# Moving the edge rows of a causal convolution from TensorE to Pool, with a rearranged start

## The chip, the cores and the metric

One core of a Trainium2 chip. The metric is the device time of one execution in microseconds (us), as the median over several runs. A program that is alone on its core has no second core to compare with, so the granted TensorE clock that each run reports is kept beside its time. A run more than 1.5% above the fastest of its kernel would count as slow and be left out. Profiles are single executions.

## The reference, cut to what matters

A lightweight causal convolution of seven taps (softmax-normalised weights, one set for each of 8 heads) is followed by a two-layer block with a cosine gate.

```python
# x (8, 4096, 192), weight (8, 7), w_in (192, 2048), w_out (2048, 192)
w = softmax(weight)                       # cut: max, exp, sum + 1e-9
x_unf = zero_padded(x)[:, idx, :]         # the row itself and the six before it
conv  = einsum('hk,bskhg->bshg', w, x_unf)    # 24 channels a head
h     = conv.reshape(32768, 192) @ w_in
out   = (h * cos(h)) @ w_out
```

## The kernel before

Tokens are taken in 64 tiles of 512; two tiles make a unit of 1024, 32 units in all. Within a tile TensorE computes eight pairs of hidden blocks (`h0` to `h7`, 6 matmuls of 512 columns each), ACT takes the cosine (`s0` to `s7`, a sine with a shifted phase), DVE multiplies, and 64 output steps (`m`, pairs of 192-column matmuls) of an earlier tile are threaded between. The convolution of a later unit (`c`, `d`) is done by TensorE with a banded matrix, in blocks of 128 tokens. The first six tokens of a block need rows of the block before it. A unit therefore has a ninth block, `UB`, into which the 16 rows around each block boundary are loaded, convolved along with the others, and copied over the wrong columns afterwards:

```python
def conv_mm(u, c, ps, i, rows, n0, n1, prev=0, **flags):        # cut
    rhs = bf[u][rows, n0:n1, h * G : (h + 1) * G]     # n1 = UB + 1: 9 blocks x 24 = 216 columns

def double_unit(u, n0=0, n1=UB + 1):                  # Pool
    nc.gpsimd.tensor_copy(out=ct[:, n0:n1, :, 1, :], in_=ct[:, n0:n1, :, 0, :])

def turn_unit(u, ...):                                # SyncE issues DMA transposes ct -> cT
def mend_edges(u):                                    # Pool, once the transposes have landed
    nc.gpsimd.tensor_copy(out=cT[u][:, 0:UB, :, 0 : K - 1],
                          in_=cT[u][:, UB]....[:, :, :, 8 : 8 + K - 1])
```

Once a unit, Pool does: mend unit u+1, cast unit u+3, double unit u+2, in this order. The first four tiles have orders of their own; this is tile 1 (`p` and `q` are the points where output banks change, and after `q` a matmul waits for a marker that SyncE passes on in its own queue):

```python
PE_ORDER  = "h0 m1 c1 m6 c2 m4 h1 m10 h2 p h3 m10 h4 m9 h5 m9 h6 m4 q h7 m11"
PE_FIRST[1] = "p m4 h0 m1 h1 m5 h2 m6 h3 m12 h4 m2 h5 m2 q m1 d1 d2 m4 h6 m6 c1 c2 m3 h7 m3"
```

## Time and profile before

| quantity | value |
|---|---|
| time | 715.81 us median of 3 runs (715.52 to 716.16) |
| TensorE busy | 704.0 of 714.0 us |
| DVE, ACT, Pool busy | 91%, 84%, 21% |
| period of a tile with convolution, without | 10.83 us, 10.46 us |

The lines behind these stand in the prediction below. A line of groups reads: source line, engine, operation, output and inputs, count; then total busy time and mean ns of one; then the idle time of the engine just before them and what ended it. In the chain and the timeline the first number is the start in us, the second the length; brackets hold the idle time before and its releaser. "L349", and "L395" in the changed kernel, is the first layer (hidden blocks); "L393" and "L439" the second. The experiments are kernels of their own with other line numbers: there a matmul `h<-cT,w` is the first layer, and `h<-x_bf,band` or `o_ps<-x_bf,band` a convolution.

### The profile page before, as it was taken

How to read it: one execution, taken by the hardware profiler on the slowest of the kernel's cores; microseconds unless marked ns; L12 is line 12 of the kernel's file. 1: busy time of each engine (PE TensorE's matmuls, PEld its weight loads, DVE VectorE, ACT ScalarE, POOL GpSimd, SP SyncE). 2: the span in 40 equal slices, each digit the busy share in tenths (PEclk: the TensorE clock that was granted, in tenths of full speed). 3: DMA queues.
4: the chain of work that ended last, by engine and by line, in shares of the span. 5: the costliest groups of instructions: out<-in, count | busy, mean ns of one | idle time of the engine just before them, and what ended most of it. 6: DMA issues, size and time to landing. Idle time of an engine off the chain costs nothing.

```text
span 714.0 us, 26320 instructions
## 1 busy us (share of the span) xinstructions
PE 704.0 (99%) x11826; PEld 539.5 (76%) x11827; DVE 647.6 (91%) x601; ACT 600.7 (84%) x718; POOL 149.4 (21%) x123
## 2 busy tenths in 40 slices
PE   7999999999999999999999999999999999999998
PEld 3577777777777777777777777777777777777776
DVE  7899999999999999999999999999999999999995
ACT  7888888888888888888888888888888888888874
POOL 5622111222102221202221122221022221121000
PEclk9999999999999999999999999999999999999999
DMA  8963554454763444553646543545644545513402
GB/s 215 233 146 85 134 146 107 113 123 97 146 134 103 129 101 119 145 123 100 141 88 133 145 108 111 129 91 145 137 90 138 103 117 146 127 50 90 95 25 68
DMA packets 183696, 85.24 MB, mean 119 GB/s; under 512 B 111648, under 2 KB 183200, under 8 KB 183584
## 3 DMA queue, kind: packets, MB, share of 16 engines
q1 hardware_dynamic: 182872, 82.59, 48.3%
q8 instruction: 92, 1.51, 0.9%
q0 software_dynamic: 416, 0.79, 0.8%
q10 hardware_dynamic: 296, 0.20, 0.1%
q14 instruction: 20, 0.16, 0.1%
HBM read 31.36 MB, written 25.17 MB: 79 GB/s over the span
## 4 chain that ended last, share of the span: by engine, by line
PE 96%; DVE 1%; ACT 1%; DMA 1%; POOL 1%; issue 0%; SPq 0%; POOLq 0%
PE o_ps L393 47%; PE h L349 45%; PE h L190 3%; DMA x_f<-in_x_dram 1%; ACT cs L356 0%; PE h L393 0%; POOL x_bf L179 0%; DVE g L360 0%; DVE band L279 0%; SPq L253 0%; POOL mask L128 0%; ACT mask L133 0%; ACT ct L298 0%; PE o_ps L190 0%; DVE diag L269 0%
## 5 line engine op out<-in xcount | busy, mean ns | idle before, releaser
L360 DVE TENSOR_TENSOR g<-h,cs 128x1024 bf16<-128x1024 f32 (+1 forms) x513 | 608.6, 1218 | 29.1 <-ACT cs L356 25.2
L356 ACT ACTIVATE cs<-h 128x1024 bf16<-128x1024 f32 (+1 forms) x513 | 514.0, 1022 | 99.8 <-PE h L349 93.7
L393 PE MATMUL o_ps<-wo,g 64*128 64x192 bf16 x8128 | 436.6, 243 | 1.2 <-ACT ct L205 0.6
L393 PEld LDWEIGHTS <-g 64*128 64x128 bf16 x8192 | 368.4, 94 | 86.6 <-SPq L164 1.1
L349 PE MATMUL h<-cT,w 64*128 64x512 bf16 (+1 forms) x3078 | 412.4, 376 | 1.9 <-DVE g L360 1.4
L349 PEld LDWEIGHTS <-w 64*128 64x128 bf16 x3078 | 161.1, 94 | 69.2 <-issue 3.4
L259 POOL COPY cT<-cT 128x144 bf16<-128x144 bf16 x31 | 9.5, 307 | 427.6 <-DMA cT<-ct 280.6
L179 POOL CAST x_bf<-x_f 128x1728 bf16<-128x1728 f32 (+1 forms) x32 | 80.4, 2514 | 8.0 <-DMA x_f<-in_x_dram 7.9
L247 POOL COPY ct<-ct 128x1728 bf16<-128x1728 bf16 x31 | 50.4, 1627 | 78.1 <-ACT ct L205 78.1
L404 DVE COPY o_sb<-o_ps 128x384 f32<-128x384 f32 x63 | 35.1, 558 | 26.1 <-PE o_ps L393 25.8
L205 ACT CAST ct<-h 128x432 bf16<-128x432 f32 x120 | 56.5, 522 | 0.6 <-PE h L190 0.3
L190 PE MATMUL h<-x_bf,band 64*128 64x216 bf16 (+1 forms) x472 | 43.4, 253 | 0.0
L404 ACT COPY o_sb<-o_ps 128x384 f32<-128x384 f32 x63 | 29.9, 474 | 1.6 <-PE o_ps L393 1.6
L190 PEld LDWEIGHTS <-band 64*128 64x128 bf16 (+1 forms) x496 | 24.3, 94 | 8.7 <-issue 1.5
L105 PE MATMUL o_ps<-zero 128*128 128x512 bf16 x12 | 4.3, 511 | 1.3 <-DVE zero L100 1.3
L105 PEld LDWEIGHTS <-zero 128*128 128x128 bf16 x15 | 1.5, 115 | 3.0 <-DVE zero L100 1.3
L414 DVE COPY o_sb<-h 128x192 f32<-128x192 f32 x1 | 0.4, 357 | 3.7 <-PE h L393 3.7
L414 ACT COPY o_sb<-h 128x192 f32<-128x192 f32 x1 | 0.3, 318 | 3.8 <-PE h L393 3.8
L461 POOL CAST wo<-wo_f 128x1536 bf16<-128x1536 f32 x2 | 2.9, 1470 | 1.8 <-DMA wo_f<-in_moe_w_out_dram 1.8
L393 PE MATMUL h<-wo,g 64*128 64x192 bf16 x64 | 3.0, 243 | 0.1
L190 PE MATMUL o_ps<-x_bf,band 128*128 128x96 bf16 (+1 forms) x24 | 1.9, 223 | 0.8 <-POOL x_bf L179 0.8
L292 PE MATMUL o_ps<-x_bf,band 128*128 128x48 bf16 x32 | 1.4, 183 | 1.2 <-ACT x_bf L179 0.7
(52 smaller groups left out, 32.3 us busy)
## 6 DMA issues: line engine op xcount, KB each, us to landing
out_dram<-o_sb SPq DMA_DIRECT2D x63, 384.0 KB
x_f<-in_x_dram SPq DMA_DIRECT2D x31, 768.0 KB
x_f<-in_x_dram SPq DMA_DIRECT2D x31, 96.0 KB
wo_f<-in_moe_w_out_dram SPq DMA_DIRECT2D x4, 384.0 KB
x_f<-in_x_dram SPq DMA_DIRECT2D x2, 384.0 KB
w<-in_moe_w_in_dram POOLq DMA_DIRECT2D x2, 384.0 KB, 6.3
cT<-ct SPq DMA_TRANSPOSE x32
out_dram<-o_sb ACTq DMA_DIRECT2D x2, 96.0 KB
```

What stands on the lines that cost most here:

```text
L105: nc.tensor.matmul(out=bank, lhsT=zero[:, 0:128], rhs=zero, start=True, stop=True)
L179: copy(out=bf[u][:, n0 + o : n1 + o, :].rearrange("p n (h k r) -> p (n h) k r", k=NC, r=R), in_=x_tiles[u][:, n0:n1, :].rearrange("p n (h ...
L190: return nc.tensor.matmul(out=ps[i // 2][:, 0 : (n1 - n0) * 2 * G].rearrange("p (n k i r) -> p i n k r", n=n1 - n0, k=NC, i=2)[:, i % 2], ...
L205: copy(o[:, :, 0, :], i[:, :, 0, :])
L247: nc.gpsimd.tensor_copy(out=ct[:, n0:n1, :, 1, :], in_=ct[:, n0:n1, :, 0, :])
L259: nc.gpsimd.tensor_copy(out=cT[u][:, 0:UB, :, 0 : K - 1], in_=cT[u][:, UB].rearrange("p c (n t) -> p n c t", t=16)[:, :, :, 8 : 8 + K - 1])
L349: nc.tensor.matmul(out=h[:, i, n0 * 128 : n1 * 128], lhsT=w[rows, k, j, :], rhs=c[rows, m0 + n0 : m0 + n1, k, :], start=(k == 0), stop=(k ...
L356: nc.scalar.activation(out=cs[:, :, part], in_=h[:, :, part], func=AF.Sin, bias=math.pi / 2.0, scale=1.0)
L360: nc.vector.tensor_tensor(out=g_tiles[t][:, 2 * j : 2 * j + 2, part], in0=h[:, :, part], in1=cs[:, :, part], op=ALU.mult)
L393: ms.append(nc.tensor.matmul(out=o_ps[tt, b, si], lhsT=g_tiles[tt][rows, f, s * 128 : (s + 1) * 128], rhs=wo[rows, f // 2, f % 2, :], star ...
L404: copies[b](o_sb[t][:, 2 * b : 2 * b + 2, :].rearrange("p s d -> p (s d)"), o_ps.pop((t, b)))
L461: nc.gpsimd.tensor_copy(out=wo[:, q * HP : (q + 1) * HP], in_=wo_f[:, q * HP : (q + 1) * HP])
```

## The change

The intent: take the ninth block off TensorE, which is the bound, and give its arithmetic to Pool, which is idle 79% of the time. Pool copies the raw edge rows into the tile that is transposed; after the transposes, tokens lie along the free axis and Pool multiplies a sliding window by the taps and adds up seven products. Unit 1 keeps the old way. The start is rearranged with it: unit 1 is loaded and cast in halves, doubled before w_out's second half is cast, and the orders of steps are changed.

```diff
@@ conv_part: 8 blocks (192 columns) from unit 2 on
+        nb = UB + (u == 1)
-            return conv_mm(u, c, ps, i, sides[rows], 0, UB + 1, ...)
+            return conv_mm(u, c, ps, i, sides[rows], 0, nb, ...)
+            if u == 2 and c == 0:
+                spread_taps(...)                    # two 7-column matmuls, once
@@ double_unit
+        nc.gpsimd.tensor_copy(out=ct[:, 0:nb, :, 1, :], in_=ct[:, 0:nb, :, 0, :])
+        for t in range(2) if u > 1 else ():
+            nc.gpsimd.tensor_copy(out=ct[:, UB, :, t, :]..., in_=bf[u][:, UB, :]...)     # raw rows
@@ mend_edges, u > 1
+        nc.gpsimd.tensor_tensor(out=edge_prod, in0=window, in1=tap..., op=ALU.mult)     # 1008 elements
+        nc.gpsimd.tensor_tensor(out=edge_prod[:, :, :, 0:3], in0=..., in1=edge_prod[:, :, :, 3:6], op=ALU.add)
+        for j in (1, 2):
+            nc.gpsimd.tensor_tensor(out=edge_prod[:, :, :, 0], in0=..., in1=edge_prod[:, :, :, j], op=ALU.add)
+        nc.gpsimd.tensor_tensor(out=cT[u][:, 0:UB, :, 0 : K - 1]..., in0=..., in1=edge_prod[:, :, :, 6]..., op=ALU.add)
@@ start
-    load_unit(1)
+    load_unit(1, 0, NB)
+    load_unit(1, NB, UB)
+    nc.gpsimd.memset(pick, 0.0)                     # and two affine_selects
-    cast_unit(1)
+    cast_unit(1, 0, NB)
+    cast_unit(1, NB)
@@ orders
-    PE_ORDER = "h0 m1 c1 m6 c2 m4 h1 m10 h2 p h3 m10 h4 m9 h5 m9 h6 m4 q h7 m11"
-    ACT_ORDER = "s0 ec1 ec2 Q s1 P s2 s3 s4 s5 s6 s7"
+    PE_ORDER = "h0 m4 c1 m6 c2 m4 h1 m7 h2 p h3 m13 h4 m10 h5 m6 h6 m3 q h7 m11"
+    ACT_ORDER = "s0 ec1 Q ec2 s1 P s2 s3 s4 s5 s6 s7"
-                "p m4 h0 m1 h1 m5 h2 m6 h3 m12 h4 m2 h5 m2 q m1 d1 d2 m4 h6 m6 c1 c2 m3 h7 m3",
+                "p h0 m5 h1 m5 h2 m6 h3 m12 h4 m2 h5 m2 q d1 d2 m5 h6 m6 c1 c2 m3 h7 m3",
@@ w_out: first half cast after unit 1's cast, second half after double_unit(1)
+            cast_wo(1)
```

(Cuts are marked by dots and by the section lines.)

More of the change, by code (lines that the diff above doesn't have):

```diff
@@ L89, with cast_wo @@
     wo_src = moe_w_out.rearrange("(i j p) d -> p j i d", i=2, p=128)
+    def cast_wo(q):
+        nc.gpsimd.tensor_copy(out=wo[:, q * HP : (q + 1) * HP], in_=wo_f[:, q * HP : (q + 1) * HP])
     def load_wo(q):
@@ L175, in cast_unit @@
     def cast_unit(u, n0=0, n1=UB + 1, copy=nc.gpsimd.tensor_copy):
-        bf[u] = xb0 if u == 0 else xbf_pool.tile([128, UB + 1, D], BF16, name="x_bf")
+        if n0 == 0:
+            bf[u] = xb0 if u == 0 else xbf_pool.tile([128, UB + 1, D], BF16, name="x_bf")
         o = 1 if u == 0 else 0
@@ L217, in conv_part @@
         ps = banks()
+        nb = UB + (u == 1)
         sides = [slice(0, 64), slice(64, 128)]
         def mm(i, rows, **flags):
-            return conv_mm(u, c, ps, i, sides[rows], 0, UB + 1, **{"start": False, "stop": False, **flags})
+            return conv_mm(u, c, ps, i, sides[rows], 0, nb, **{"start": False, "stop": False, **flags})
         if whole:
             for i in range(4):
-                conv_mm(u, c, ps, i, slice(0, 128), 0, UB + 1, start=i % 2 == 0, stop=i % 2 == 1)
+                conv_mm(u, c, ps, i, slice(0, 128), 0, nb, start=i % 2 == 0, stop=i % 2 == 1)
+            if u == 2 and c == 0:
+                spread_taps(ps[1][:, UB * 2 * G : UB * 2 * G + K])
             yield
@@ L239, in conv_part, with double_unit @@
         for b in range(2):
-            conv_out(u, c, ps, 0, 0, UB + 1, nc.scalar.copy, banks=(b,))
+            conv_out(u, c, ps, 0, 0, nb, nc.scalar.copy, banks=(b,))
+            if b and u == 2 and c == 0:
+                nc.scalar.copy(tap, ps[1][:, UB * 2 * G : UB * 2 * G + K])
             yield
     cT = {}
-    def double_unit(u, n0=0, n1=UB + 1):
+    def double_unit(u):
         ct = ct_tiles[u]
-        nc.gpsimd.tensor_copy(out=ct[:, n0:n1, :, 1, :], in_=ct[:, n0:n1, :, 0, :])
+        nb = UB + (u == 1)
+        nc.gpsimd.tensor_copy(out=ct[:, 0:nb, :, 1, :], in_=ct[:, 0:nb, :, 0, :])
+        for t in range(2) if u > 1 else ():
+            nc.gpsimd.tensor_copy(out=ct[:, UB, :, t, :].rearrange("p k (h r) -> p k h r", r=R),
+                                  in_=bf[u][:, UB, :].rearrange("p (h k r) -> p k h r", k=NC, r=R))
     def turn_unit(u, n0=0, n1=UB + 1):
@@ L255, in turn_unit, with spread_taps @@
         cT.pop(u - 2, None)
-    def mend_edges(u):
-        nc.gpsimd.tensor_copy(out=cT[u][:, 0:UB, :, 0 : K - 1],
-                              in_=cT[u][:, UB].rearrange("p c (n t) -> p n c t", t=16)[:, :, :, 8 : 8 + K - 1])
+    tap = consts.tile([128, K], FP32)
+    pick = consts.tile([128, 2, 2, 4, 2, R], BF16)
+    def spread_taps(ps):
+        for i in range(2):
+            nc.tensor.matmul(out=ps, lhsT=pick[:, i].rearrange("p t q i r -> p (t q i r)"), rhs=wn[:, i, :],
+                             start=i == 0, stop=i == 1, skip_group_check=True)
+    edge_prod = consts.tile([128, NC * UB, K - 1, K], FP32)
+    def mend_edges(u):
+        if u == 1:
+            nc.gpsimd.tensor_copy(out=cT[u][:, 0:UB, :, 0 : K - 1],
+                                  in_=cT[u][:, UB].rearrange("p c (n t) -> p n c t", t=16)[:, :, :, 8 : 8 + K - 1])
+            return
+        raw = cT[u][:, UB].rearrange("p c (n t) -> p (c n) t", t=16)
+        window = raw[:, :, 2 : 2 + K]
+        window = bass.AP(window.tensor, window.offset, [*window.ap[:2], [1, K - 1], [1, K]])
+        nc.gpsimd.tensor_tensor(out=edge_prod, in0=window,
+                                in1=tap.rearrange("p (a b k) -> p a b k", a=1, b=1).to_broadcast([128, NC * UB, K - 1, K]),
+                                op=ALU.mult)
+        nc.gpsimd.tensor_tensor(out=edge_prod[:, :, :, 0:3], in0=edge_prod[:, :, :, 0:3], in1=edge_prod[:, :, :, 3:6], op=ALU.add)
+        for j in (1, 2):
+            nc.gpsimd.tensor_tensor(out=edge_prod[:, :, :, 0], in0=edge_prod[:, :, :, 0], in1=edge_prod[:, :, :, j], op=ALU.add)
+        nc.gpsimd.tensor_tensor(out=cT[u][:, 0:UB, :, 0 : K - 1].rearrange("p n c t -> p c n t"),
+                                in0=edge_prod[:, :, :, 0].rearrange("p (c n) t -> p c n t", c=NC),
+                                in1=edge_prod[:, :, :, 6].rearrange("p (c n) t -> p c n t", c=NC), op=ALU.add)
     cast_unit(0, 0, NB, nc.scalar.copy)
@@ L281 @@
     cast_unit(0, NB, UB)
+    nc.gpsimd.memset(pick, 0.0)
+    for i in range(2):
+        nc.gpsimd.affine_select(out=pick[:, i, :, :, i, :], in_=pick[:, i, :, :, i, :], compare_op=ALU.not_equal, fill=1.0,
+                                base=0, pattern=[[0, 2], [-32, 4], [0, R]], channel_multiplier=1)
     ct_tiles[0] = ct_pool.tile([128, UB + 1, NC, 2, 64], BF16, name="ct")
@@ L459, in flush @@
                         load_edges(2)
-                        for q in range(2):
-                            nc.gpsimd.tensor_copy(out=wo[:, q * HP : (q + 1) * HP], in_=wo_f[:, q * HP : (q + 1) * HP])
+                        cast_wo(0)
                 elif k[0] == "s" and t < NT:
```

## The prediction

> **What bounds the kernel now.** I read the engine shares first, then the chain that ended last, then the costliest groups, then the busy time in windows, and last the timeline of the start. From the page's first and fourth parts:
>
> ```profile
> PE 704.0 (99%) x11826; PEld 539.5 (76%) x11827; DVE 647.6 (91%) x601; ACT 600.7 (84%) x718; POOL 149.4 (21%) x123
> PE 96%; DVE 1%; ACT 1%; DMA 1%; POOL 1%; issue 0%; SPq 0%; POOLq 0%
> ```
>
> TensorE is busy 704.0 of 714.0 us and holds 96% of the chain, so only TensorE work taken away, or its roughly 10 idle us, can pay. The windows view says where those 10 us are (columns: window, its length, then busy us of PE, PEld, DVE, ACT, POOL, clock, DMA share, GB/s):
>
> ```profile
> 10.00:20.00 10.00, 8.06 (x81) 4.15 (x79) 8.83 (x11) 8.69 (x14) 5.16 (x3) 1.00 1.17 290
> 20.00:30.00 10.00, 8.62 (x118) 5.36 (x118) 8.63 (x9) 8.10 (x11) 7.38 (x4) 1.00 1.22 260
> 30.00:40.00 10.00, 9.52 (x152) 6.65 (x148) 7.85 (x8) 9.32 (x14) 2.67 (x3) 1.00 0.95 184
> 300.00:400.00 100.00, 100.00 (x1701) 77.25 (x1697) 92.36 (x84) 85.35 (x102) 22.67 (x17) 1.00 0.50 120
> ```
>
> From 40 us until about 702 us TensorE never stops; the idle time is in the first 40 us and the last 12. The chain in order of time gives the period of one 512-token tile, by the start of the same pair of hidden blocks in successive tiles:
>
> ```profile
> 643.17 1.29 PE h L349 x12
> ...
> 654.00 1.29 PE h L349 x12
> ...
> 664.46 1.29 PE h L349 x12
> ...
> 674.92 1.30 PE h L349 x12
> ```
>
> With convolution a tile takes 654.00 - 643.17 = 10.83 us; in the last four tiles, where none is left, 674.92 - 664.46 = 10.46 us. Convolution therefore costs 0.37 us a tile. A tile has 8 convolution matmuls in 4 pairs (two row halves run together): 0.37/4 = 92.5 ns a pair of 216 columns. The durations printed for matmuls overlap and are not this cost; these are the groups I use:
>
> ```profile
> L360 DVE TENSOR_TENSOR g<-h,cs 128x1024 bf16<-128x1024 f32 (+1 forms) x513 | 608.6, 1218 | 29.1 <-ACT cs L356 25.2
> L259 POOL COPY cT<-cT 128x144 bf16<-128x144 bf16 x31 | 9.5, 307 | 427.6 <-DMA cT<-ct 280.6
> L179 POOL CAST x_bf<-x_f 128x1728 bf16<-128x1728 f32 (+1 forms) x32 | 80.4, 2514 | 8.0 <-DMA x_f<-in_x_dram 7.9
> L247 POOL COPY ct<-ct 128x1728 bf16<-128x1728 bf16 x31 | 50.4, 1627 | 78.1 <-ACT ct L205 78.1
> L205 ACT CAST ct<-h 128x432 bf16<-128x432 f32 x120 | 56.5, 522 | 0.6 <-PE h L190 0.3
> L190 PE MATMUL h<-x_bf,band 64*128 64x216 bf16 (+1 forms) x472 | 43.4, 253 | 0.0
> ```
>
> **What the Trainium skill says.** "TensorE: Matmul & The Clock Gate", section Back-to-back issue gap, gives N/2.4 + 2.5 ns for a warm matmul of N columns. The trace agrees: 216 columns give 92.5 ns, as measured; and a tile without convolution is 24 pairs of 512 columns (215.8 ns) and 64 pairs of 192 (82.5 ns), together 10.46 us, again as measured. The 64 pairs also show that 192-column pairs keep this pace with a weight load each. "GPSIMD Engine Reference", section 3.1, gives 2.6 cycles an element for a two-input operation (4497 ns for 2048); no two-input Pool operation is in this trace. "SBUF — State Buffer" says Pool contends with a DVE instruction that has two SBUF inputs or runs in a two-port mode. DVE's product here has one PSUM and one SBUF input, and its 1024-element form lasts at most 1226 ns, median 1224, with Pool casts running beside many of them: it agrees that there is no contention to fear.
>
> **The change part by part.**
>
> (a) Removed from TensorE. For units 2 to 31 the ninth block (the 16 edge rows of each 128-token block of a unit) leaves the convolution: 216 columns become 192. A pair then costs 192/2.4 + 2.5 = 82.5 ns, 10.0 less. Tiles 2 to 59 each have 4 pairs: 58 x 4 x 10.0 = 2.32 us. Unit 2 is convolved in tile 1 by 8 full-height matmuls: 8 x 10 = 0.08 us. Sum 2.40 us, all on the path, since TensorE has no gap there. Tiles should become 10.79 us.
>
> (b) Added to TensorE: two matmuls of 7 columns once, to spread the taps over partitions; with their weight loads I take 0.1 to 0.15 us.
>
> (c) ACT. Evacuations fall from 432 to 384 elements: 522 to about 474 ns (the 384-element output copy's time in this trace), so ACT does about 58 x 2 x 0.048 = 5.6 us less; plus one small tap copy. Off the path.
>
> (d) Pool. From the two copies, (1627 - 307)/(1728 - 144) = 0.833 ns an element and 187 ns fixed. Doubling 1536 elements: 1.47 us. Two raw edge copies of 192: 0.35 us each. Mending: a product of 1008 at 2.2 ns an element plus 0.2, 2.4 us; an addition of 432, 1.1; three of 144 at 0.5, 1.5; in all 5.0 us in place of 0.307. All these are estimates (2.2 ns is the GPSIMD page's rate). A unit goes from 4.5 to about 9.7 us of Pool in 21.6. Pool busy becomes about 305 us. Is it hidden? In a middle unit the mend starts at 344.16, when the transposes land, and its first reader is the tile that begins at 358.02. Pool's order is mend, cast, double: 349.2, 351.7, 353.2, raw copies 353.9. The convolution that reads the cast starts near 358.7, the next transposes at 359.63. So 5.7 us are left, 4.5 in the unit that lands latest (410.33, which is 1.2 late against the three units before it). Hidden.
>
> (e) The start. These lines of the timeline (start, length, engine, idle before) matter:
>
> ```profile
> 17.38 0.53 PE L190 MATMUL o_ps<-x_bf,band 128*128 128x216 bf16 x4 [0.80 <-POOL x_bf L179]
> ...
> 21.85 0.82 PE L349 MATMUL h<-cT,w 64*128 64x512 bf16 x6
> ...
> 29.05 0.26 PE L393 MATMUL o_ps<-wo,g 64*128 64x192 bf16 x2 [0.56 <-SPq L164]
> ```
>
> Casting unit 1 in halves puts its first half ahead of the landing of the second: but Pool now first makes the pick matrix (a fill and two selects, about 1 us after 13.2), so I expect the cast to end near 17.0 instead of 17.3. That shortens the 0.80 us wait, which pays little: ACT works without a break from 14.9 to 22.1 and is the bound of tile 0. Next, tile 1's first hidden block at 21.85 waited for the transposes of unit 0 (TensorE's weight loader idle 0.36 us on that DMA), which nothing here hastens. The four output matmul pairs that stood before it now follow: 4 x 82.5 = 0.33 us lost. At 29.05 the pair that waited 0.56 us for a queue marker on SyncE, stuck behind the issue of unit 1's transposes (23.58 to 28.94), is now behind unit 2's convolution, whose input was cast by 28.0: the 0.56 us are filled. Doubling unit 1 ahead of the second cast of w_out starts at ACT's end, 21.2, instead of 21.93; the transposes are issued 0.7 us earlier, but the DMA share is over 1 from 20 to 30 us, so I count nothing. Net: 0.56 - 0.33 = 0.23 gained, less 0.1 to 0.15 for the taps: about 0.1 us. Later waits, such as 0.48 us for DVE at 36.52, shift along.
>
> (f) The steady order of output matmuls is rearranged with the same 64 a tile: no work saved or added.
>
> **Sum:** 2.40 + 0.1 gives 2.5 us; I add 0.1 for the earlier transposes, should they land a little sooner. 715.81 - 2.6 = 713.2 us, a ratio of 0.9964.
>
> **The rivals.**
> 1. Pool becomes a wait. The small strided runs (6 and 7 elements) could make its operations twice as slow as I say: mending 10 us. Mend, cast and double would then end near 359, at the transposes' start, and the late units would push transposes back, yet mending still starts some 8 us or more before its reader. For it: section 7 of the GPSIMD page puts reads with a step over 8 bytes at 2.9 cycles an element against 1.9, and three of the additions step by 28 bytes. Against: the slack above, and Pool at 45%. If it came true over all 29 units with 1 us of wait each, the time would be near 742; a stray wait or two, 714.5.
> 2. DVE becomes the bound. A tile holds 8 x 1.224 + 0.558 = 10.35 us of DVE; at 10.79 it is 96% busy. TensorE would wait for hidden banks if the new order bunches its blocks. Against: the order before ran with no TensorE gap, and ACT gets lighter. With 20 ns a tile, 1.2 us are lost: 714.4.
> 3. The start pays more than I count: the transposes of unit 1 land 0.7 us earlier, and the waits at 17.38, 29.05 and 36.52 all go. Then 1 us more: 712.2.
> 4. The start pays nothing, or loses the 0.33 us: 713.5.
>
> **Range and chances.** The 2.40 us is arithmetic on a saturated engine; the start is worth -0.4 to +1.2; a steady wait costs up to 1.2. That gives 712.2 to 714.4 for 8 times in 10. Two per cent is 14.3 us: TensorE's work cannot fall so far, and only the full form of rival 1 could be slower by so much.
>
> **What would show it.** (a) Tiles of 10.79 us in the chain, the convolution group at 64x192, no TensorE idle from 40 to 702 us. (d) Pool's group of products near 2.4 us, mending near 5 us a unit, Pool busy near 305 us, and no TensorE or SyncE wait put down to Pool in the steady part. (c) ACT evacuations near 474 ns. (e) The 0.56 us wait for SyncE gone; TensorE idle in the first 40 us down by a few tenths only. I am wrong if tiles keep 10.83 us (the columns were not the bound), if Pool's chain shows ahead of a transposition, or if TensorE's first 40 us change by over 1 us.

## The result, and the profile after

The changed kernel took 713.65 us as the median of 6 runs (712.96 to 715.70), the kernel before 715.88 us in the runs beside them. The ratio is 0.9972, with a 95% interval of 0.9959 to 0.9985: the mean time of one kernel's fast runs over that of the other's of the same rounds, so not quite the ratio of the medians.

The profiled run happened to be the slowest of the six: 715.70 us, span 714.0 us, granted clock 0.998. The other five had spans of 711.3 to 712.3 us. First the engine shares and the chain by engine, after:

```profile
PE 703.3 (99%) x11828; PEld 538.3 (75%) x11829; DVE 646.7 (91%) x601; ACT 590.4 (83%) x719; POOL 300.9 (42%) x307
PE 96%; DVE 1%; DMA 1%; ACT 1%; issue 0%; POOL 0%; POOLq 0%; SPq 0%
```

Pool is busy twice as long and holds 0% of the chain (1% before). Then the chain in order of time, from the same pair of hidden blocks in tile 3 on:

```profile
49.66 1.30 PE h L395 x12
...
653.89 1.30 PE h L395 x12
...
664.36 1.29 PE h L395 x12
...
674.81 1.30 PE h L395 x12
```

and tile 3's pair in the kernel before:

```profile
47.52 1.29 PE h L349 x12
```

A tile with convolution now takes 10.79 us: (653.89 - 49.66)/56, from tile 3 to tile 59. The tiles at the end, without convolution, still take 10.46 us, within 0.01. The windows view, with the columns of before:

```profile
10.00:20.00 10.00, 8.04 (x80) 4.03 (x78) 8.77 (x11) 8.63 (x14) 6.07 (x7) 1.00 1.24 292
20.00:30.00 10.00, 7.98 (x96) 5.08 (x98) 6.92 (x7) 6.36 (x9) 6.12 (x4) 0.83 1.05 244
30.00:40.00 10.00, 9.10 (x140) 6.21 (x136) 7.76 (x8) 9.13 (x15) 4.37 (x5) 1.00 0.94 167
300.00:400.00 100.00, 100.00 (x1710) 77.28 (x1706) 92.58 (x84) 84.09 (x102) 47.75 (x47) 1.00 0.50 120
```

TensorE is full in the middle as before; from 20 to 30 us the clock was only 0.83, and it did 96 matmuls where the kernel before did 118. Finer windows of the same trace, and the lines of the timeline around them:

```profile
22.00:23.00 1.00, 0.53 (x4) 0.27 (x6) 0.79 (x1) 0.18 (x1) 1.00 (x2) 0.82 0.81 237
23.00:26.00 3.00, 3.00 (x24) 1.70 (x22) 1.52 (x2) 1.09 (x2) 1.35 (x1) 0.50 1.06 311
26.00:29.00 3.00, 3.00 (x58) 2.29 (x54) 2.15 (x3) 2.70 (x3) 2.56 (x1) 0.99 1.28 225
```

```profile
16.85 0.53 PE L194 MATMUL o_ps<-x_bf,band 128*128 128x216 bf16 x4 [0.20 <-DVE ct L207]
18.03 0.82 PE L395 MATMUL h<-cT,w 64*128 64x512 bf16 x6 [0.65 <-DVE g L406]
...
22.47 1.34 PE L395 MATMUL h<-cT,w 64*128 64x512 bf16 x6 [2.02 <-DMA cT<-ct]
```

Tile 1's first hidden block waited 2.02 us for unit 0's transposes, now with no output steps ahead of it. Just after it, the clock fell to 0.50: half-microsecond windows have 0.64 from 22.5 to 23.0 and 0.95 from 26.0 to 26.5, which puts the fall at about 22.64 and the return at about 26.05. The block's six matmuls took 1.34 us instead of 0.82. The groups of the changed work:

```profile
L292 POOL TENSOR_TENSOR edge_prod<-cT,tap 128x1008 f32<-128x1008 bf16 x30 | 67.2, 2239 | 347.0 <-DMA cT<-ct 347.0
L209 ACT CAST ct<-h 128x384 bf16<-128x384 f32 x120 | 51.8, 483 | 8.5 <-PE h L194 4.8
L194 PE MATMUL h<-x_bf,band 64*128 64x192 bf16 (+1 forms) x472 | 41.0, 243 | 0.0
L297 POOL TENSOR_TENSOR edge_prod<-edge_prod 128x144 f32<-128x144 f32 x60 | 33.3, 554 | 4.7
L295 POOL TENSOR_TENSOR edge_prod<-edge_prod 128x432 f32<-128x432 f32 x30 | 30.3, 1009 | 2.4
L298 POOL TENSOR_TENSOR cT<-edge_prod 128x144 bf16<-128x144 f32 x30 | 18.3, 608 | 2.4
```

The product waits 347.0 us in 30 units for transposes to land: Pool arrives early in all of them.

So the trace already divides the result. From tile 3's pair (47.52 before, 49.66 after) to tile 59's (654.00 and 653.89) the changed kernel gained 2.25 us; up to tile 3 this particular run lost 2.14 us.

### The profile page after: what moved, and what is told of

It reads as the page before. It is cut to its first block, busy times and chain, and to the rows that moved or that the text cites. A ratio compares the mean times of both kernels' runs of the same rounds, so it can differ in the third digit from the quotient of the medians.

```text
span 714.0 us, 26519 instructions
## 1 busy us (share of the span) xinstructions
PE 703.3 (99%) x11828; PEld 538.3 (75%) x11829; DVE 646.7 (91%) x601; ACT 590.4 (83%) x719; POOL 300.9 (42%) x307
## 4 chain that ended last, share of the span: by engine, by line
PE 96%; DVE 1%; DMA 1%; ACT 1%; issue 0%; POOL 0%; POOLq 0%; SPq 0%
PE o_ps L439 47%; PE h L395 46%; PE h L194 3%; DMA cT<-ct 1%; DVE g L406 0%; ACT cs L402 0%; PE h L439 0%; DVE band L320 0%; POOL mask L131 0%; ACT mask L136 0%; ACT ct L343 0%; PE o_ps L194 0%; DVE diag L309 0%; DVE cT L361 0%; PE h L358 0%
## 5 line engine op out<-in xcount | busy, mean ns | idle before, releaser
L406 DVE TENSOR_TENSOR g<-h,cs 128x1024 bf16<-128x1024 f32 (+1 forms) x513 | 606.4, 1220 | 32.3 <-ACT cs L402 21.8
L292 POOL TENSOR_TENSOR edge_prod<-cT,tap 128x1008 f32<-128x1008 bf16 x30 | 67.2, 2239 | 347.0 <-DMA cT<-ct 347.0
L183 POOL CAST x_bf<-x_f 128x1728 bf16<-128x1728 f32 (+2 forms) x33 | 80.6, 2444 | 6.7 <-DMA x_f<-in_x_dram 6.7
L209 ACT CAST ct<-h 128x384 bf16<-128x384 f32 x120 | 51.8, 483 | 8.5 <-PE h L194 4.8
L258 POOL COPY ct<-ct 128x1536 bf16<-128x1536 bf16 (+1 forms) x31 | 45.6, 1472 | 3.4 <-ACT ct L209 3.4
L194 PE MATMUL h<-x_bf,band 64*128 64x192 bf16 (+1 forms) x472 | 41.0, 243 | 0.0
L297 POOL TENSOR_TENSOR edge_prod<-edge_prod 128x144 f32<-128x144 f32 x60 | 33.3, 554 | 4.7
L295 POOL TENSOR_TENSOR edge_prod<-edge_prod 128x432 f32<-128x432 f32 x30 | 30.3, 1009 | 2.4
L298 POOL TENSOR_TENSOR cT<-edge_prod 128x144 bf16<-128x144 f32 x30 | 18.3, 608 | 2.4
L260 POOL COPY ct<-x_bf 128x192 bf16<-128x192 bf16 x60 | 19.2, 349 | 0.0
```

The lines of the kernel that those rows point to most:

```text
L183: copy(out=bf[u][:, n0 + o : n1 + o, :].rearrange("p n (h k r) -> p (n h) k r", k=NC, r=R), in_=x_tiles[u][:, n0:n1, :].rearrange("p n (h ...
L194: return nc.tensor.matmul(out=ps[i // 2][:, 0 : (n1 - n0) * 2 * G].rearrange("p (n k i r) -> p i n k r", n=n1 - n0, k=NC, i=2)[:, i % 2], ...
L209: copy(o[:, :, 0, :], i[:, :, 0, :])
L258: nc.gpsimd.tensor_copy(out=ct[:, 0:nb, :, 1, :], in_=ct[:, 0:nb, :, 0, :])
L292: nc.gpsimd.tensor_tensor(out=edge_prod, in0=window, in1=tap.rearrange("p (a b k) -> p a b k", a=1, b=1).to_broadcast([128, NC * UB, K - 1 ...
L295: nc.gpsimd.tensor_tensor(out=edge_prod[:, :, :, 0:3], in0=edge_prod[:, :, :, 0:3], in1=edge_prod[:, :, :, 3:6], op=ALU.add)
```

## The experiments

Two questions: does the gain come from the edges alone, and what is the start worth; and how much more could Pool carry. Each table line of times gives the median and range. In the first call the kernel before had a median of 715.98 us, with one run of 719.29 at a clock of 0.997.

### The start alone

The kernel before, with the new start and nothing of the edges:

```diff
-    load_unit(1)
+    load_unit(1, 0, NB)
+    load_unit(1, NB, UB)
-    cast_unit(1)
+    cast_unit(1, 0, NB)
+    cast_unit(1, NB)
-  "p m4 h0 m1 h1 m5 ... h5 m2 q m1 d1 d2 m4 h6 ..."
+  "p h0 m5 h1 m5 ... h5 m2 q d1 d2 m5 h6 ..."
+            cast_wo(1)                 # after double_unit(1) instead of before
```

> The kernel before with only the new start: unit 1 loaded and cast in halves, doubled ahead of w_out's second cast, and tile 1's new order; convolution and edges as before. Theory A (the new order leaves TensorE without work before tile 1's first hidden block, and the clock falls when that gap grows): tiles stay 10.83 us, the gap is 1 to 2 us with the wait put down to the transposes, granted clock under 1.000 in some runs, times scattered from 715 to 718, median near 716, ratio about 1.000. Rival B (the new start gains by itself, and the dip in the changed kernel's profile was chance): no dip, median near 715.3, spread under 0.6 us.

Measured: 715.77 us (715.46 to 716.12), ratio 1.0001 (0.9988 to 1.0013), clock 1.000 in all five runs. The timeline of TensorE:

```profile
16.69 0.53 PE L194 MATMUL o_ps<-x_bf,band 128*128 128x216 bf16 x4 [0.20 <-DVE ct L207]
17.87 0.82 PE L355 MATMUL h<-cT,w 64*128 64x512 bf16 x6 [0.65 <-DVE g L366]
...
21.95 0.82 PE L355 MATMUL h<-cT,w 64*128 64x512 bf16 x6 [1.65 <-DMA cT<-ct]
28.58 0.54 PE L194 MATMUL h<-x_bf,band 128*128 128x216 bf16 x4
30.05 0.82 PE L355 MATMUL h<-cT,w 64*128 64x512 bf16 x6 [0.27 <-DVE g L366]
```

Every wait that the new start takes away comes back as another. Unit 1's convolution waits 0.20 us instead of 0.80, and the next hidden block then waits 0.65 us for DVE to free its buffer. The marker wait of 0.56 us at 29.05 is filled by unit 2's convolution, and the block behind it waits 0.27 us for DVE and starts at 30.05, exactly when it did before. Doubling began at 21.15 instead of 21.93, yet unit 1's transposed edges were ready at 32.47, against 32.40. Tile 3's pair stands at 47.53, against 47.52: the start is worth nothing. Both theories missed in part: there was a gap of 1.65 us but no clock dip and no scatter.

### The edges alone

The changed kernel with all three points of the old start.

```diff
-    load_unit(1, 0, NB) ...            +    load_unit(1)
-    cast_unit(1, 0, NB) ...            +    cast_unit(1)
-  "p h0 m5 h1 m5 ... q d1 d2 m5 ..."   +  "p m4 h0 m1 h1 m5 ... q m1 d1 d2 m4 ..."
-            cast_wo(1)                 # after double_unit(1)
+                        cast_wo(1)     # straight after cast_wo(0)
```

> The changed kernel's edges on Pool and its steady order, with the start of the kernel before in all three points. Theory A: tiles of 10.79 us, no clock under 1.000, runs within 0.6 us of each other, median near 713.6 (715.88 less 2.4, plus 0.15 for the taps). Rival C (Pool's added set-up, or its edge work, spoils the start): clock dips and scatter as in the changed kernel, median 714 or more.

Measured: 713.71 us (713.25 to 714.72), ratio 0.9973 (0.9960 to 0.9985), beside 0.9972 for the changed kernel. Clock 1.000 throughout. Its tile 3 pair is at 47.34 and its tile 59 pair at 651.58: 10.79 us a tile. The edges carry all of the gain that these runs can tell. The scatter of 1.5 us was not expected by theory A.

### Four output steps put back ahead of the first hidden block

```diff
-  "p h0 m5 h1 m5 h2 m6 h3 m12 h4 m2 h5 m2 q d1 d2 m5 h6 m6 c1 c2 m3 h7 m3"
+  "p m4 h0 m1 h1 m5 h2 m6 h3 m12 h4 m2 h5 m2 q m1 d1 d2 m4 h6 m6 c1 c2 m3 h7 m3"
```

> The changed kernel with tile 1's old order alone: four output pairs' steps stand before the first hidden block again, one after the marker. Theory A: the 2 us gap is split in two, no clock under 1.000 in any run, spread under 0.8 us, median 713.3 or less. Rival B or C: dips and scatter as in the changed kernel, median near 713.7.

Measured: 713.74 us (713.07 to 714.43), ratio 0.9969 (0.9955 to 0.9983), clocks 0.999 and 1.000. No dip, as expected, but the scatter stayed at 1.4 us, and the expected median of 713.3 us or less was missed. In its profiled run unit 0's transposes took 3.12 us to issue, the first hidden block started at 22.39, and the wait for the marker was 0.97 us.

### Matmuls on zeros in the gap

```diff
-  "p h0 m5 ..."
+  "p w h0 m5 ..."
+            elif k[0] == "w":
+                keep_warm(5, o_pools[1].tile([128, T], FP32, name="o_ps1"))
```

> The changed kernel with five matmuls on zeros into a free output bank ahead of tile 1's first hidden block (the results are not used). Theory A: the clock stays at 1.000 in every run, spread under 0.8 us, best runs no faster than the changed kernel's best, median near 712.9. Rival (the clock has nothing to do with the gap): dips as often as in the changed kernel, or a median over 713.7.

Measured: 713.92 us (713.83 to 713.99), ratio 0.9974 (0.9962 to 0.9987). The tightest of all, with no dip, but not faster: in its trace the zeros ran up to the first hidden block, which started at 22.33, and 0.46 us of marker wait appeared at 29.95. The expected 712.9 us was a miss; the median even lies over the 713.7 us that the rival had named, but of the rival's dips there was none.

### The changed kernel again

No edit. In this call the kernel before had a median of 715.87 us over 11 runs, with 718.81 at a clock of 0.998 among them.

> The changed kernel unaltered, to stand beside its variants on one chip and to see whether its scatter and its clock dip come back. Theory A' (the edges save 2.5 us; the new start is worth about 0; where unit 0's second transposes land late the start is up to 1 us worse, and now and then the clock falls for 3.4 us, which costs some 1.6 more): median 713.4 to 714.0, range over 1 us, perhaps one run over 715. Rival: the first run's 715.7 was chance, all runs within 0.5 us.

Measured: 713.46 us (713.04 to 715.44), ratio 0.9969 (0.9953 to 0.9986). One run of six again stood out, 715.44 us, and it alone had a low clock, 0.997. The profiled run this time had none (713.44 us):

```profile
21.96 0.82 PE L395 MATMUL h<-cT,w 64*128 64x512 bf16 x6 [1.70 <-DMA cT<-ct]
```

With that, tile 3's pair is at 47.47, so against the dipped run (49.66) the start differs by 2.19 us. The first hidden block is 0.51 us earlier, which leaves 1.68 us. Half the clock for 3.4 us of work is 1.7 us, so the clock accounts for it to within the waits that follow, which differ by 0.14 us in sum.

### Unit 1 loaded and cast whole

```diff
-    load_unit(1, 0, NB)
-    load_unit(1, NB, UB)
+    load_unit(1)
-    cast_unit(1, 0, NB)
-    cast_unit(1, NB)
+    cast_unit(1)
```

> The changed kernel with unit 1 loaded and cast whole again, the rest of its start kept. Theory A': the cast ends 0.7 us later, near 17.4 us, which costs nothing because ACT is the bound there: median within 0.3 us of the changed kernel. If the extra transfer is what makes unit 0's transposes late (theory D), they land by 21.9 us and the runs lie within 0.6 us of each other, median near 713.3. Rival (the halves pay): 714.2 or more.

Measured: 713.56 us (713.03 to 715.68), ratio 0.9971 (0.9955 to 0.9988), two runs of 715.11 and 715.68 us at a clock of 0.998. The halves pay nothing and do no harm that these runs show. Theory D is refuted: unit 0's transposes still took 2.69 us to issue, the first hidden block started at 21.99, and the runs span 2.7 us.

### The old steps ahead, the convolution behind the marker

```diff
-    load_unit(1, 0, NB) ... cast_unit(1, 0, NB) ...
+    load_unit(1) ... cast_unit(1)
-  "p h0 m5 h1 m5 h2 m6 h3 m12 h4 m2 h5 m2 q d1 d2 m5 h6 m6 c1 c2 m3 h7 m3"
+  "p m4 h0 m1 h1 m5 h2 m6 h3 m12 h4 m2 h5 m2 q d1 d2 m5 h6 m6 c1 c2 m3 h7 m3"
```

> The changed kernel's edges and early doubling, unit 1 whole, and in tile 1 the four old output steps ahead of the first hidden block but unit 2's convolution straight after the marker. Theory A': the 0.56 us wait is filled without the 0.33 us loss; part of it comes back as a wait for DVE before the seventh hidden block, so 0.2 to 0.3 us better than edges_only: median 713.4, best runs near 713.0. Rival (DVE gives all of it back): equal to edges_only within 0.1 us in the trace's start.

Measured: 713.20 us (712.90 to 713.48), ratio 0.9960 (0.9947 to 0.9973), no clock under 0.999. Two lines of its timeline:

```profile
21.83 0.82 PE L393 MATMUL h<-cT,w 64*128 64x512 bf16 x6 [0.15 <-DMA cT<-ct]
...
29.86 0.82 PE L393 MATMUL h<-cT,w 64*128 64x512 bf16 x6 [0.24 <-DVE g L404]
```

The first gap is mostly filled, but 0.24 us comes back as a wait for DVE. Tile 3's pair is at 47.27, 0.07 us better than the edges alone: in the trace's start it is the rival that held (equal within 0.1 us), not the 0.2 to 0.3 us of theory A'. Its runs span 0.6 us where the changed kernel's beside it span 2.4. The intervals of the two ratios overlap, so it is not shown to be faster; it is the steadier of the two in these runs.

### The old steady order

```diff
-    PE_ORDER = "h0 m4 c1 m6 c2 m4 h1 m7 h2 p h3 m13 h4 m10 h5 m6 h6 m3 q h7 m11"
-    ACT_ORDER = "s0 ec1 Q ec2 s1 P s2 s3 s4 s5 s6 s7"
+    PE_ORDER = "h0 m1 c1 m6 c2 m4 h1 m10 h2 p h3 m10 h4 m9 h5 m9 h6 m4 q h7 m11"
+    ACT_ORDER = "s0 ec1 ec2 Q s1 P s2 s3 s4 s5 s6 s7"
```

> The changed kernel with the steady order of output steps and evacuations of the kernel before. Theory A' (the order does no work, and TensorE has slack against DVE either way): tiles of 10.79 us, median within 0.3 us of the changed kernel. Rival (the order was needed, since a shorter convolution lets TensorE run into DVE's buffers): TensorE waits put down to DVE in the steady part, tiles of 10.80 to 10.83 us, median 714.3 to 716.

Measured: 713.37 us (712.99 to 713.69), ratio 0.9961 (0.9948 to 0.9974). TensorE was busy 615.00 of the 615.00 us from 40 to 655 us. The rearrangement of the steady order is worth nothing that these runs show.

The start differs from trace to trace, and at the two ends of this table with unit 0's transposes (the three in the middle are alike). The kernels of this table that begin tile 1 with the hidden block:

| kernel | issue of unit 0's transposes, us | first hidden block of tile 1 starts | tile 3's pair starts |
|---|---|---|---|
| old steady order | 1.96 | 21.52 | 47.03 |
| start alone (216 columns) | 2.45 | 21.95 | 47.53 |
| unit 1 whole | 2.69 | 21.99 | 47.50 |
| changed kernel, again | 2.85 | 21.96 | 47.47 |
| changed kernel, first profile | 3.16 | 22.47 | 49.66, with the clock dip |

### Pool's product three times over

In this call the kernel before had a median of 715.71 us.

```diff
+        for _ in range(3):
             nc.gpsimd.tensor_tensor(out=edge_prod, in0=window, in1=tap..., op=ALU.mult)
```

> The changed kernel with Pool's 1008-element product done three times (same result), 2 x 2.24 = 4.5 us more Pool work a unit. Theory P (transposes, mend, cast, doubling and raw copies form one loop a unit: 6.4 + 5.3 + 2.6 + 2.1 = 16.4 us of a period of 21.58, so 5.2 us are free): the loop is 20.9 us, nothing shows, median within 0.5 us of the changed kernel, tiles 10.79 us. Rival (the slack is only the gap to the next transposes, 5.7 us in a middle unit but 4.3 in the late ones): single waits of TensorE on DMA, some us more.

Measured: 719.42 us (719.03 to 720.58), ratio 1.0049 (1.0032 to 1.0065). The chain by engine, and then Pool's work in one unit and the issue of transposes behind it, from the timeline:

```profile
POOL 38%; PE 37%; DMA 21%; issue 2%; DVE 1%; ACT 1%; SPq 0%; POOLq 0%
```

```profile
348.71 6.88 POOL L293 TENSOR_TENSOR edge_prod<-cT,tap 128x1008 f32<-128x1008 bf16 x3 [6.12 <-DMA cT<-ct]
...
361.06 1.50 POOL L258 COPY ct<-ct 128x1536 bf16<-128x1536 bf16 x1
362.47 0.67 POOL L260 COPY ct<-x_bf 128x192 bf16<-128x192 bf16 x2
363.17 4.69 SPq L267 DMA_TRANSPOSE cT<-ct  x1
```

The raw copies end at 363.14 and the transposes start at 363.17, where in the changed kernel they wait for something else: the loop closes. My sum of it (20.9 us), and with it the expected "nothing shows", was wrong. From the product's start to the end of the copies it is 14.43 us here and 14.49 on average (every fourth unit has a fill of 0.25 us besides), and in the 24 units that the trace's listing showed, the transposes took 7.25 us on average from issue to landing (taken as the start of the product that waits for them), not the 6.4 of the one unit I had looked at. Together 21.74 us, over the period of 21.58; the products' starts are 21.80 us apart on average. The rival had the size ("some us more") but as single waits: in 25 of 28 units the transposes start within 0.1 us of the end of the copies, so it is the loop. Over 29 units 0.22 us each is 6.4 us, and the measured loss against the changed kernel's 713.46 is 6.0.

### Pool's product five times over

```diff
+        for _ in range(5):
             nc.gpsimd.tensor_tensor(out=edge_prod, in0=window, in1=tap..., op=ALU.mult)
```

> The same product done five times, 9.0 us more a unit. Theory P: the loop is 25.4 us, 3.8 over the period of 21.58, so after the slack of the first units is used each unit takes about 25.4 us: about 25 to 29 units x 3.8 us gives 95 to 110 us more, 808 to 824 us, TensorE waiting for transposes or mended edges. Rival (only the mend's own reader counts, 13.9 us away from its start in the kernel before): no loss, 714 us.

Measured: 839.34 us (837.67 and 841.00), ratio 1.1721 (1.1684 to 1.1757). The chain by engine:

```profile
POOL 60%; DMA 23%; PE 13%; issue 3%; DVE 1%; ACT 1%; POOLq 0%; SPq 0%
```

The products start 25.85 us apart. (25.85 - 21.58) x 29 = 124 us, against 839.34 - 713.46 = 126. The loop theory holds, but the expected 808 to 824 us was too low: landing took 6.8 us on average, not 6.4, which makes the excess 4.3 us a unit and not 3.8. The granted clock fell as well, to 0.949 and 0.959 on average; TensorE holds only 13% of the chain here.

### A gap made long, and the same gap filled

The transposes of unit 0's second half are issued twice with the same result. The second kernel has 16 matmuls on zeros in the gap besides.

```diff
+        for _ in range(2 if u == 0 else 1):
             nc.sync.dma_start_transpose(out=cT[u]..., in_=ct...)
```

> The changed kernel with unit 0's second transposes issued twice (same result), so that tile 1's first hidden block comes 2.5 to 5 us later and TensorE idles 4 to 7 us before it. Theory A (an idle TensorE of about 2 us or more there lets the clock fall to half for one stretch of 3.4 us): granted clock near 0.5 from about the block's start, in every run; time up by the delay plus about 1.7 us. Rival (the dip has another cause): clock 1.000, time up by the delay alone.

> As gap_long, with sixteen matmuls on zeros (3.5 us) into a free output bank in the gap. Theory A: the clock stays at or near 1.000, and the time is 1 to 2 us less than gap_long's at the same delay. Rival: no difference.

Measured: with the bare gap 719.86 us (718.35 to 720.56), clocks 0.994, 0.995, 0.994 and 0.998; with the zeros 717.55 us (717.16 to 720.90), clocks 1.000, 0.999 and 0.999, and 0.998 in the run of 720.90. Windows of the first:

```profile
24.00:27.00 3.00, 0.62 (x4) 0.28 (x6) 0.11 (x1) 0.00 (x0) 1.03 (x1) 0.63 0.91 184
27.00:31.00 4.00, 4.00 (x34) 2.27 (x32) 1.23 (x1) 2.05 (x2) 0.56 (x1) 0.50 1.07 319
31.00:34.00 3.00, 3.00 (x50) 2.10 (x48) 2.26 (x2) 1.97 (x2) 2.58 (x2) 0.90 1.24 234
```

and of the second, with zeros:

```profile
27.00:31.00 4.00, 4.00 (x68) 2.85 (x66) 3.39 (x3) 3.65 (x4) 1.16 (x1) 1.00 1.17 307
```

At half the clock TensorE did 34 matmuls in 4 us, at the full clock 68. Tile 3's pair is at 54.43 without the zeros and 51.45 with them; 0.69 us of that is a later first block (26.38 against 25.69), and the other 2.3 us fits the clock: it was at half from 24.77 to 31.59 us, two times the expected 3.4, and TensorE worked at half for 5.2 us of it. So an idle gap does bring the clock down, and filling it with useless work avoids that in the profiled run and, by their clocks, in two of the other three. The traces and clocks show this; the times alone do not (ratios 1.0045, 1.0025 to 1.0065, and 1.0030, 1.0004 to 1.0057, overlap).

The kept traces show more than the length of a gap. Within each, the changes of the granted clock lie whole multiples of 3.41 us apart (in the product five times over at 23.70, 27.11, 61.25, 64.66, 112.45 us and so on). Cut into stretches of 3.41 us at these steps, TensorE's busy time in the stretch ahead of a fall was 0.00 to 1.49 us (at most 44%) in all 19 falls while the kernels ran: one in the first profile of the changed kernel (1.39 us), one with the bare gap, 17 in the product five times over. No stretch at full clock with 1.53 us (45%) or more was followed by a fall. In these traces, then, it is not the length of a gap alone: where it lies against the steps decides too.

## Why the prediction was right, and where it was not

**(a) The columns.** Right to the digit. Predicted 10.79 us a tile; measured 10.79. Predicted 2.32 us for 58 tiles; measured 2.25 us over the 56 periods between tile 3 and tile 59, which is 0.040 us each and gives 2.33 for 58. The medians agree: 715.88 - 713.65 = 2.23 us in all, where 2.6 was predicted. The start of the kernel with the edges alone gave no more than 0.2 us beside it.

**(b) The taps.** Predicted 0.1 to 0.15 us; in the trace the two matmuls start at 31.12 and the next step at 31.25, 0.13 us later.

**(c) ACT.** Predicted 474 ns an evacuation, measured 483. ACT's total fell by 10.3 us, of which 4.7 are the evacuations' group (5.6 predicted); where the rest comes from was not looked into. Off the path, as said.

**(d) Pool.** The durations held: product 2.24 us (2.4 predicted), 432-element addition 1.01 (1.1), 144-element ones 0.55, 0.55 and 0.61 (0.5 each), mending 5.28 in all with the short gaps between its five operations (5.0), Pool's total 300.9 us (305). It was hidden, as said. The step that was mis-sized is the slack, "So 5.7 us are left, 4.5 in the unit that lands latest". I measured it from one unit's landing, and as a distance to the next transposes. (At 344.16, which I read as the landing, the trace names a hidden block of TensorE as the releaser, as for 10 of the 31 mends.) It is a loop that must close once a unit: 7.06 us of transposes on average, and 9.77 us of Pool from the product's start to the end of the copies (10.06 in every fourth unit), make 16.8 of 21.58 us, so about 4.7 us are free. The changed kernel's trace has it directly: the copies end 3.60 to 5.74 us ahead of the next transposes, 4.62 on average. The product three times over shows it: 4.6 us more of Pool just overran it. Rival 1 had supposed mending of 10 us to cost "a stray wait or two, 714.5", or 742 with 1 us a unit; with 9.9 us of mending the kernel took 719.4, because the loop exceeded its period by 0.2 us a unit on average.

**(e) The start.** "Net: 0.56 - 0.33 = 0.23 gained, less 0.1 to 0.15 for the taps: about 0.1 us" failed in its first term. The 0.56 us wait was indeed filled, but the buffer behind it was not free earlier, and 0.27 us came back as a wait for DVE; the start alone gave 715.77 against 715.98 us and a ratio of 1.0001. What was said of the halves (the cast ends earlier, and it pays little) and of the transposes ("I count nothing") held; the 0.1 us that the sum then adds for them after all did not come. Rival 3, a start worth 1 us more, fell; rival 4, a start that pays nothing, is what the runs show. The prediction named a change of over 1 us in TensorE's first 40 us as a sign of being wrong: in the dipped profile tile 3's pair came 2.14 us later than before, so the sign came true there, and not in the second profile (47.47 against 47.52). The prediction did not see that the new order strips TensorE of work in the longest wait of the start, nor what a clock that falls would cost there: two of the changed kernel's twelve runs took 715.7 and 715.4 us, outside the range of 712.2 to 714.4, at clocks of 0.998 and 0.997. The median lay within it.

**(f) The order.** No gain and no loss, as said; the old order ran equally full.

**Rival 2**, DVE as the bound, fell: TensorE had no idle time between 40 and 702 us. Nor did the doubled Pool work slow DVE: its 1024-element product took 1222 ns on average, 1220 before.

**What stays open.** How often the new order of tile 1 brings a dip is not measured. Three kernels with the edges on Pool and the hidden block first had them in 4 of 24 runs (the changed kernel twice in 12, unit 1 whole twice in 6, the old steady order never in 6); the product three times over, with the same start, in 1 of 4; the start alone in none of 5; the three with the old steps ahead in none of 16.

The traces show why it can: sliding a stretch of 3.41 us over the time from 8 to 30 us of each, TensorE's share in the emptiest one is 38% and 41% in the two profiles of the changed kernel, 33% to 57% in the other five kernels with the hidden block first and the gap as it is, but 60% to 64% in the kernel before, the three with the old steps ahead and the two with zeros, where no placing comes down to the 44% that went ahead of falls.

But the kernel before also had runs of 719.29, 718.81 and 717.51 us at clocks of 0.997 to 0.998, and others of 717.15 and 717.55 us at 1.000; none of these was traced. That a fall of the clock follows a long gap there is shown by the two kernels made for it and by one trace. Why unit 0's transposes take between 1.96 and 3.16 us to issue, and tile 1's first block starts up to a microsecond apart, was not found; loading unit 1 in one piece or two does not decide it.

## What to carry to other kernels

When one engine is full, price a change by the columns it takes off that engine's stream; moving 24 of 216 columns to an idle engine paid just their time, and nothing that was done to the waits of the start paid anything that these runs show; where a trace was followed, the next buffer or marker was waiting behind. Check the engine that receives the work as a loop (all that must happen once a period, with the average time of its transfers), not by the gap seen in one period. And in a start-up, do not leave TensorE without work in its longest wait, since half a clock for 3.4 us of work costs 1.7 us, more than half of what the whole change gains. (Filling it with zeros did not make this kernel faster, though: 713.92 us.)

## What the Trainium skill lacked or had wrong

- "TensorE: Matmul & The Clock Gate", section Why this matters for your kernels, says to leave no idle gaps over about 3 us between bursts. Here the clock fell after a gap of 2.02 us: the 3.4 us ahead of the fall held some 1.4 us of matmuls by the trace, and the half clock then lasted from about 22.64 to 26.05 us. Gaps of 1.65 and 1.70 us in other runs were without it. In the 19 falls of all traces the stretch ahead held up to 1.49 us of matmuls, so TensorE need not be idle throughout.
- "GPSIMD Engine Reference", section 3.1, gives 2.6 cycles (2.17 ns at the 1.2 GHz of its example) an element for two inputs. The 1008-element product, bf16 by fp32 with an overlapping window and a broadcast, took 2239 ns: with 187 ns fixed (an estimate from the two copies of the kernel before) that is 2.04 ns an element. Section 7 has 2.9 cycles for reads that step over 8 bytes; additions of two inputs that step by 28 bytes took 554 ns for 144 elements, by the same estimate 2.55 ns or 3.1 cycles, and no page has the two-input case.
- Pages give a time for one block of 128 by 128 and bandwidths for DMA transposes; none gives the time from issue to landing of a transposition like this one on this chip (27 such blocks, from SBUF to SBUF, beside other transfers): 6.09 to 7.92 us in the 24 units listed of the changed kernel, 7.06 on average, taken to the start of the product that waits for it. That average, not the best case, decides a loop.
